# One tag per place: each tile goes where the kernel's own list schedule put it

## The chip, the cores and the metric

The kernel runs on one core of one Trainium2 chip. The metric is the device time of one execution in microseconds (us), as the median of several runs. The engines are named as in the profile: PE (TensorE, the matmuls; PEld its weight loads), DVE (VectorE), ACT (ScalarE), POOL (GpSimd) and SP (SyncE, which issues nearly all transfers here). PE writes its results into PSUM, which has eight banks of 2 KB per partition. All other tiles lie in SBUF.

## The reference

The input x has 2048 rows of 1024 bfloat16 numbers. Two layers with the same weights follow each other. A layer is an attention block A and then a feed-forward block B, each with a layer norm in front and a residual around it:

```
x = x + A(layernorm(x));  x = x + B(layernorm(x))        (twice)

A: qkv = x @ wqkv; 32 heads of 32 numbers
   position s looks at the 8 positions s, s-2, ..., s-14 (those that exist)
   o = softmax(q.k / sqrt(32)) v;  return o @ wo
B: h = relu(x @ w1 + b1)**2;  return h @ w2 + b2          (w1: 1024 x 3584)
```

## The kernel before

**Tiling.** A dilation of 2 keeps even and odd rows apart, so the rows are split by parity and worked on in blocks of 512: four blocks a layer, eight block steps u = 0 to 7 in all. A step has these stages: `SA` loads the rows and does the first layer norm; `SQ` or `SQ7` makes q, k and v; `S2` does the attention products on DVE; `SW` multiplies with wo, adds the residual (`xm`) and does the second layer norm; `SF1` and `SF2` are the two halves of the feed-forward block. Stages of neighbouring steps are interleaved: the attention of step u+1 runs on DVE while PE does the feed-forward block of step u.

**Seven products instead of eight.** From step 3 (q, k, v) and step 1 (feed-forward) on, a product of 2 x 2 blocks is made with seven block products, which share sums held in PSUM banks X, Y and Z (`product`; the matmul is line 572). Between products ACT copies a bank to SBUF, because the next product goes on adding to the same bank: a copy of X is a tile `u` (line 531 for q, k and v, lines 1060 and 1064 for the feed-forward block), a copy of Y or Z is `yq` (line 535) or `y` (line 1070). PE can't start the next product in that bank before the copy has been read out of it. DVE then adds `u` and `yq` (line 539). The combined weights are made once from the raw ones, in the early steps (`keep_w1`, `keep_wqkv` with tiles `tr` and `tv`, lines 464 and 469, and `keep_w2`), and are written to memory, from which later steps load them.

**Results.** `out_tile` adds a finished bank to `xm`: ACT copies the bank into a tile `yxo` (line 957), DVE adds and writes a tile `xo` (line 958), and SP stores `xo` to memory, to `xs` after the first layer and to the output after the second (line 353).

**What sets the order.** Nothing is left to an automatic scheduler. Every operation is recorded in a `Plan` with its engine, an estimated duration, a priority and the tiles that it reads and writes. `Plan.schedule` is a list scheduler: it goes forward in modelled time and gives each free engine its ready operation of the lowest priority number. The result is one order for all engines, in which `Plan.emit` then writes the instructions. On the chip each engine works through its own instructions in that order. Where one needs another engine's result, or a place that another tile still holds, it waits, and all behind it on its engine wait too. That holds for SP as well: a transfer that has to wait for its place holds back the transfers behind it.

**Places.** SBUF is divided into places of fixed sizes by class: 3 of 8304 bytes ("8Q": q, k, v), 11 of 8 KB ("8K": weights `w`, `xnA`, `xnB`, `o`, `s1`, T and TA), 6 of 4 KB, 12 of 2 KB ("2K": rows, `tr`, `tv`, `rr`), 9 of 1 KB ("1K": `u`, `y`, `yq`, `yxo`, `yxa`, `yxm`, `xo`), and some small ones. PSUM is the class "ps" with 8 places. The list scheduler keeps a list of free places for each class and starts an operation only when a place is free for each of its new tiles. It takes the place that has been free longest, and gives it back when the last user is done:

```python
b.slot = free[b.cls].pop(0)        # when the first user of tile b starts
free[b.cls].append(b.slot)         # when the last user of tile b is done
```

For a transfer, "done" is the end of its turn in a modelled queue of transfers (`DMA_MBS`, 0.38 MB a us) plus `DMA_LAT`, 2.2 us (or 4 us for the stores of combined weights). The number `b.slot` serves the plan alone. `place`, which `emit` calls when it writes the first instruction of a tile, asks a tile pool for the tile by the name of its class, with as many buffers as the class has places. The pool then chooses the place by its own rule as the instructions are written, and places the waits that this needs. So plan and program can differ in which tile follows which in a place.

Of the kernel before, what the change touches and what calls it, by code (L numbers as in the profile page):

```python
# [100 lines left out]
class Plan:  # L101
# [150 lines left out]
    def emit(self, place):  # L252
        self.shift(ORDER)
        order, self.timed = self.schedule()
        for o in order:
            for b in o.bufs:
                if b.tile is None:
                    b.tile = place(b)
            o.fn()

class _Kernel:
# [76 lines left out]

    def place(self, b):
        pool = self.psum if b.cls == "ps" else self.arena  # L340
        return pool.tile(b.shape, b.dt, name=b.tag, tag=b.cls, bufs=self.p.classes[b.cls][0])

    def nxt(self):
        self.seq += 1
# [995 lines left out]
```

## Time and profile before

| | us |
|---|---|
| median of 3 runs | 1171.28 |
| the three runs | 1168.42, 1171.89, 1171.28 |
| the profiled execution | 1168.59 |
| its span, first to last instruction | 1166.5 |

| in the span | busy | share | instructions |
|---|---|---|---|
| PE | 1145.8 us | 98% | 7572 |
| PEld | 767.6 us | 66% | 7623 |
| DVE | 1015.1 us | 87% | 1778 |
| ACT | 785.3 us | 67% | 1531 |
| 16 DMA engines, SP's queue | | 89.0% | 356.79 MB in all queues |

A wait in the profile is told as "engine, tile and line <- what ended it". A time of a matmul is modelled at its end, and neighbouring matmuls overlap, so the busy time of a group of matmuls is a little longer than the distance of their starts. A transfer is shown on its issuing queue (SPq) by the time of its issue. The time to its landing is counted from that issue. The granted clock is 1.00 where PE runs at full rate.

### The profile page before, as it was taken

Reading aid. Unit: us, or ns where it says so; the run is one execution under the profiler, and the core shown is the slowest. Engines: PE = TensorE matmul, PEld = TensorE weight load, DVE = VectorE, ACT = ScalarE, POOL = GpSimd, SP = SyncE. Lnnn points to the kernel's source line nnn. Section 1 sums busy time; section 2 is a strip of 40 time slices with the busy share of each in tenths; the row PEclk is TensorE's granted clock in tenths of the full one; section 3 lists DMA queues with packets and bytes.
Section 4 is the critical chain, followed back from the end, with each engine's and each line's share of the span. In section 5 each row is a group of like instructions: output and inputs, shape, how many; then the busy total and the mean of one; then the engine's idle time right before and its main releaser. Section 6 shows DMA issues by size and latency. Waiting matters only on the chain. (4 is left out here: it accounts for less than half of the span.)

```text
span 1166.5 us, 20203 instructions
## 1 busy us (share of the span) xinstructions
PE 1145.8 (98%) x7572; PEld 767.6 (66%) x7623; DVE 1015.1 (87%) x1778; ACT 785.3 (67%) x1531; POOL 1.8 (0%) x8
## 2 busy tenths in 40 slices
PE   8999999999999999999999999998999999999998
PEld 6565544557846787468864688555885568844864
DVE  4899999779999999959999699995999879998551
ACT  5743795565984689756894669845698376943771
POOL 0000000000000000000000000000000000000000
PEclk9999999999999999999999999999999999999999
DMA  9789999899999797997989797996979979787882
GB/s 353 215 238 285 348 282 313 292 315 343 379 327 382 230 382 256 342 383 237 371 287 372 263 358 272 298 395 209 368 258 323 406 246 386 248 327 273 294 291 90
DMA packets 196539, 356.79 MB, mean 306 GB/s; under 512 B 63834, under 2 KB 134874, under 8 KB 177242
## 3 DMA queue, kind: packets, MB, share of 16 engines
q1 hardware_dynamic: 196154, 354.99, 89.0%
q8 instruction: 59, 0.97, 0.3%
q10 hardware_dynamic: 288, 0.52, 0.1%
q14 instruction: 38, 0.31, 0.1%
HBM read 307.76 MB, written 39.58 MB: 298 GB/s over the span
## 5 line engine op out<-in xcount | busy, mean ns | idle before, releaser
L572 PEld LDWEIGHTS <-w 128*128 128x128 bf16 (+1 forms) x4424 | 433.3, 98 | 71.3 <-issue 10.6
L1153 PEld LDWEIGHTS <-r 128*128 128x128 f16 x1183 | 115.7, 98 | 134.4 <-ACT r L1091 0.8
L1153 PE MATMUL X<-w,r 128*128 128x512 f16 (+2 forms) x787 | 177.3, 377 | 0.3
L852 DVE TENSOR_TENSOR P<-q,k 128x2048 f16<-128x2048 f16 x128 | 154.1, 1223 | 12.4 <-ACT q L778 12.1
L931 DVE TENSOR_TENSOR pr<-pb,v 128x2048 f16<-128x2048 f16 x128 | 154.8, 1221 | 0.0
L572 PE MATMUL X<-T,w 128*128 128x256 f16 x1176 | 146.4, 273 | 0.2
L937 DVE TENSOR_TENSOR pr<-pr 128x512 f16<-128x512 f16 (+1 forms) x256 | 132.3, 550 | 0.0
L860 DVE TENSOR_TENSOR P<-P,P 128x2048 f16<-128x2048 f16 x102 | 123.7, 1217 | 0.1
L801 PE MATMUL pq<-xnA,w 128*128 128x512 f16 x528 | 118.0, 379 | 0.0
L982 PE MATMUL py<-w,o 128*128 128x512 bf16 x492 | 113.7, 380 | 3.1 <-ACT py L421 1.9
L1091 ACT ACTIVATE r<-rr 128x1024 f16<-128x1024 f16 x98 | 107.7, 1128 | 0.8 <-DVE rr L1083 0.5
L801 PEld LDWEIGHTS <-w 128*128 128x128 bf16 x528 | 75.3, 144 | 37.8
L572 PE MATMUL X<-TA,w 128*128 128x256 f16 x720 | 91.1, 274 | 5.3 <-ACT u L531 5.3
L982 PEld LDWEIGHTS <-o 128*128 128x128 bf16 x512 | 50.3, 98 | 59.0 <-issue 2.5
L531 ACT CAST u<-X 128x512 f16<-128x512 f32 x90 | 51.8, 589 | 46.2 <-PE X L572 32.8
L1074 DVE TENSOR_TENSOR rr<-u,y 128x512 f16<-128x512 f16 x147 | 60.9, 422 | 24.1 <-ACT y L1070 12.6
L1070 ACT CAST y<-Z 128x512 f16<-128x512 f32 x98 | 60.1, 637 | 14.3 <-PE Z L572 14.0
L643 DVE BATCH_NORM_STATS2 bs<-xm 128x6 f32<-128x512 f16 x64 | 43.9, 689 | 26.4 <-ACT xm L988 26.2
L1060 ACT CAST u<-X 128x512 f16<-128x512 f32 x105 | 62.5, 632 | 3.4 <-PE X L572 3.3
L988 ACT CAST xm<-py 128x512 f16<-128x512 f32 x52 | 30.5, 587 | 38.5 <-PE py L982 34.6
L572 PE MATMUL Z<-xnB,w 128*128 128x256 f16 x392 | 50.8, 273 | 0.0
L572 PE MATMUL Y<-xnB,w 128*128 128x256 f16 x392 | 50.6, 273 | 0.0
(133 smaller groups left out, 1629.9 us busy)
## 6 DMA issues: line engine op xcount, KB each, us to landing
w<-w1s SPq DMA_DIRECT2D x84, 1024.0 KB, 8.6
w<-tw SPq DMA_DIRECT2D x56, 896.0 KB, 6.5
w<-in_B_w_dram SPq DMA_DIRECT2D x42, 896.0 KB, 6.4
w<-wqqv SPq DMA_DIRECT2D x35, 1024.0 KB, 7.6
w<-in_A_wqkv_dram SPq DMA_DIRECT2D x18, 1024.0 KB, 8.6
w<-in_A_wo_dram SPq DMA_DIRECT2D x16, 1024.0 KB, 8.2
w<-wqk SPq DMA_DIRECT2D x15, 1024.0 KB, 8.5
w<-in_B_w_dram SPq DMA_DIRECT2D x28, 512.0 KB, 7.5
```

What stands on the lines that cost most here:

```text
L572: nc.tensor.matmul(bank[:, a, :], lw[:, k, left(a)], rhs(k), start=(start and k == 0 and a == 0), stop=(k == 3), skip_group_check=True)
L801: nc.tensor.matmul(pq[:], wv[:, kd % 4, c0:D:8], xnT[:, :, kd, :], start=(kd == 0), stop=(kd == KD - 1))
L852: nc.vector.tensor_tensor(cur[:], q[:, c, None, hb * HB:(hb + 1) * HB].to_broadcast([128, W, HB]), _win_ap(k[:, c, :], HALO + hb * HB, HB) ...
L860: nc.vector.tensor_tensor(other[:], other[:], cur[:], ALU.add)
L931: p.add("DVE", dve(2048), lambda pr=pr, ch=ch: nc.vector.tensor_tensor(pr[:], pb[:], _win_ap(v[:, ch, :], HALO + hb * HB, HB), ALU.mult), ...
L937: nc.vector.tensor_tensor(dst, pr[:, 0:n, :], pr[:, n:2 * n, :], ALU.add)
L982: nc.tensor.matmul(py[:], o[:, c, tl * 128:(tl + 1) * 128], wos[c // 4][:].rearrange("p (a b) n -> p a (b n)", a=4)[:, c % 4, db * 512:(db ...
L1060: p.add("ACT", act(512), lambda: nc.scalar.copy(us[i][:], X[:]), [(X, 0)], [(us[i], 0), (us[i], 1)], UP, name="u")
L1070: p.add("ACT", act(512), lambda: nc.scalar.copy(y[:], bank[:]), [(bank, 0)], [(y, 0)], 1.5, name="y")
L1074: p.add("DVE", dve(512), lambda: nc.vector.tensor_tensor(r[:, :, m, :], us[i][:], y[:], ALU.add), [(us[i], 0), (us[i], 1), (y, 0)], [(r, ( ...
L1091: p.add("ACT", act(1024), lambda: nc.scalar.activation(out=r2[:, f:f + 2, :].rearrange("p a t -> p (a t)"), in_=r[:].rearrange("p a m t -> ...
L1153: nc.tensor.matmul(banks[q][:, lo:hi], left(jj, q), w[:, j, lo:hi], start=(start and jj == 0), stop=(jj == h - 1), skip_group_check=True)
```

## The change

`place` now asks for the tile by a tag that names the class and the number `b.slot` that the list schedule gave the tile, with one buffer for each such tag. So the pool has nothing left to choose: each tile goes to the place that the plan gave it. The sizes and the number of places stay as they are. Their addresses in SBUF change, because the places are laid out in the order of their first use instead of class by class. The plan itself is not changed.

```diff
     def place(self, b):
         pool = self.psum if b.cls == "ps" else self.arena
-        return pool.tile(b.shape, b.dt, name=b.tag, tag=b.cls, bufs=self.p.classes[b.cls][0])
+        return pool.tile(b.shape, b.dt, name=b.tag, tag=f"{b.cls}.{b.slot}", bufs=1)
```

## The prediction

> **What bounds the kernel now.** I read the page's busy shares first, then who TensorE (PE) waits for, then the timeline around each of those waits, then windows over them, and last the tile view of the buffer found there. The page:
>
> ```profile
> PE 1145.8 (98%) x7572; PEld 767.6 (66%) x7623; DVE 1015.1 (87%) x1778; ACT 785.3 (67%) x1531; POOL 1.8 (0%) x8
> ```
>
> PE is busy for 98% of a span of 1166.5 us. Little can be won, and only where PE stands. The chain that ended last names matmuls almost alone. Next, the waits of PE alone (total, times, longest):
>
> ```profile
> PE X L572 <- ACT u L531: 5.3, 4, 2.1
> PE Z L572 <- ACT yq L535: 3.8, 1, 3.8
> PE py L982 <- ACT py L421: 1.9, 3, 0.7
> PE pt L717 <- DVE xn L699: 1.8, 1, 1.8
> ...
> PE Y L1153 <- ACT r L1091: 0.3, 1, 0.3
> ```
>
> No transfer is in this list: PE never waits for weights. The first two rows are five stalls. In each, PE wants a PSUM bank that ScalarE (ACT) has not copied out. Timeline of ACT at these five places; the bracket is its idle time and what ended it:
>
> ```profile
> 372.75 0.59 ACT L531 CAST u<-X 128x512 f16<-128x512 f32 x1 [2.68 <-DMA xs<-xo]
> ...
> 512.83 0.59 ACT L531 CAST u<-X 128x512 f16<-128x512 f32 x1 [2.16 <-DMA xs<-xo]
> ...
> 646.87 1.07 ACT L531 CAST u<-X 128x512 f16<-128x512 f32 x2 [2.18 <-DMA xs<-xo]
> ...
> 790.67 0.59 ACT L957 CAST yxo<-X 128x512 f16<-128x512 f32 x1 [5.06 <-DMA out_dram<-xo]
> ...
> 932.90 0.59 ACT L531 CAST u<-X 128x512 f16<-128x512 f32 x1 [4.34 <-DMA out_dram<-xo]
> ```
>
> The copy writes a 1 KB tile (u or yxo) into a place that an xo tile still holds, because its store to memory has not landed. The copy needs nothing from that store but the place. How slow the stores are, from the tile view of xo:
>
> ```profile
> DMA to landing us min/median/max: 1.6/5.3/10.9
> ```
>
> What one stall costs, from PE's timeline:
>
> ```profile
> 786.57 1.04 PE L572 MATMUL Y<-xnA,w 128*128 128x256 f16 x8
> 787.44 1.04 PE L572 MATMUL X<-TA,w 128*128 128x256 f16 x8
> ...
> 792.28 1.01 PE L572 MATMUL Z<-xnA,w 128*128 128x256 f16 x6 [3.81 <-ACT yq L535]
> ```
>
> Eight such matmuls start 0.87 us after the eight before (787.44 - 786.57). The next eight could start at 788.31 and start at 792.28: 3.97 us lost. There is a second loss behind it, in windows over the stall, the stretch after it, and the stall at 931 (PE, PEld, DVE, ACT, POOL, granted clock, DMA share, GB/s):
>
> ```profile
> 788.30:792.20 3.90, 0.17 (x2) 0.00 (x1) 0.00 (x0) 1.53 (x4) 0.00 (x0) 1.00 1.06 432
> 792.80:796.10 3.30, 3.08 (x15) 2.02 (x15) 0.83 (x3) 1.58 (x3) 0.00 (x0) 0.50 0.65 230
> ...
> 931.30:933.50 2.20, 0.13 (x2) 0.00 (x0) 0.00 (x0) 0.60 (x2) 0.00 (x0) 1.00 0.99 417
> ```
>
> After the stall of 3.97 us the granted clock is 0.50; the trace's clock records put that at 3.41 us. VectorE (DVE) has nothing to do in either stall: it is starved by them, not their cause.
>
> **The change part by part.** *Removed: five waits for a store.* By the rule of 787.44 above the losses of PE are: 370.92 + 0.87 = 371.79 to 373.39, 1.60; 511.58 + 0.87 = 512.45 to 513.47, 1.02; 645.54 + 0.87 = 646.41 to 647.50, 1.09; 3.97; 930.39 + 0.87 = 931.26 to 933.54, 2.28. Sum 9.96 us. All of it is on the path, since PE is the path.
>
> Do they go? The two built programs have the same instructions in the same order on every engine; waits and addresses differ. I laid the built addresses over the times of this trace. Of 2319 tiles that follow another tile in a place, 450 follow a different one. The five copies now follow tiles last read at 370.33, 510.20, 643.25, 785.86 and 929.02, all by DVE, no store. ACT became idle (start less bracket) at 370.07, 510.67, 644.69, 785.61 and 928.56, and the bank to be copied was complete at 370.21, 510.87, 644.83, long before, and 928.81. The latest of the three, plus 0.6 us, ends the copy at 370.9, 511.5, 645.4, 786.5 and 929.6, ahead of PE's 371.79, 512.45, 646.41, 788.31 and 931.26. At 788 PE needs the third of three copies, 0.48 us apart in the timeline: 787.5, a margin of 0.8 us, the smallest of the five. So all five go.
>
> *Removed with them: the slow clock.* 3.41 us at half rate do the work of 1.71 us: 1.7 us lost. The stall of 2.28 us left the clock at 1.00, so it goes even if the long stall only shrinks to that.
>
> *Late next.* Three copies stand on a store with little to spare before (0.25, 0.43 and 0.71 us after its landing); they move too. Over all 1 KB tiles the closest that the list's places come to a landed store, at these times, is 2.6 us (an xo written at 785.44).
>
> *Added: waits at the list's own places.* In 16 cases the tile now ahead in the place is still in use at the time of the write. Three kinds. (a) Seven weight loads from SP take the place of a tile that PE reads until 0.83 us (six) or 0.51 us (one) after the old issue. SP stands, and the loads, stores and transposes behind it in its queue stand too. Between 0, since these weights land 6.3 to 18.4 us ahead of their first reader, and 6 x 0.83 + 0.51 = 5.5 us if that lead were gone. I take 0: the lead is measured. (b) Where weights are combined and kept, 187 to 247 us: one ACT copy is 1.40 us late, two DVE operations 1.52 and 0.27, with PSUM copies queued behind the first and combinations behind the others. PE's three stalls there (239 to 252 us) sum to 0.87 + 0.59 + 0.89 = 2.35 us and end with ACT's seeding copies. Between -2.35, if other waits of ACT go and take these along, and +3.2. I take 0: the late copy is 50 us ahead of them, and the late DVE work does not end them. (c) Six ACT and DVE writes of 0.09 to 0.57 us: 0 to 0.6 for the one at 934, behind a stall that goes; the others are within 0.1. I take 0.
>
> *Sum.* The profiled execution took 1168.59 us (span 1166.5 and 2.1 around it). 1168.6 - 9.96 - 1.7 = 1156.9 us. It lies 2.7 us below the median of 1171.28 (runs 1168.42 to 1171.89). If those 2.7 us are stalls of these kinds they go too, if not they stay; I add 1.1 and say 1158.0.
>
> A rule that speaks against this: the Trainium skill, SBUF — State Buffer, "The DMA setup-cost knee", says that a transfer costs about a fixed 2 us plus its bytes over 436 GB/s. By it an xo store of 128 KB would take an estimated 2.3 us, the one issued at 780.92 would have left its place before 785.61, no copy would ever wait, and the change would be worth nothing: 1168.6. The trace disagrees: the copy at 790.67, 9.7 us after that issue, is released by its landing.
>
> **The rivals.** *New waits take back part.* For it: the kernel plans its list with 2.2 us to a landing (DMA_LAT) behind a modelled queue, where stores here take up to 10.9, so the list too can give a place that is not free. Against it: the rows under (a) to (c), and the nearest store at 2.6 us. All bounds at once are 5.5 + 3.2 + 0.6 = 9.3 us: 1166.2.
>
> *No gain: another resource sets the pace where the stalls were.* DVE is the candidate, at 87% overall and 98.6% busy from 260 to 371 us. Against it: 0.51 us of DVE work in 9.7 us of the five stalls. If PE ran into DVE each time, the time would stay at 1168.6. The same time results if the program does not do what it says, which the built addresses exclude.
>
> *Slower: the transfers become the bound.* From 376 to 1012 us the 16 DMA engines are 0.86 to 0.91 busy outside the stalls. Without 11.7 us of 641 the share becomes 0.88 to 0.93. The point is 1.0: if the moved places made the transfers there take 12% longer (570 us of work to 641), PE would start to wait for weights, and at 15% (656 us) the time would be 1168.6 + 15 = 1183. For it: the share reaches 1.03 in 260 to 371 us. Against it: PE loses 0.2 us in that very stretch.
>
> **How the numbers follow.** As forecast 0.72 (1154.5 to 1160); new waits take back part 0.14 (1160 to 1166); no gain 0.06 (1167.8 to 1174.8); slower 0.08. Range 1154.5 to 1166: the lower end is 1156.9 less the 2.35 of (b), the upper the bound of the first rival; it holds 0.86. A measurement of this kernel tells about 0.3%, 3.5 us, from no change: faster 0.86, same 0.06, slower 0.08.
>
> **What would show it.** Right: no transfer of xo among the releasers of ACT's u, yq and yxo copies; PE's rows for u and yq gone from its waits, or under 1 us; no clock of 0.50 between the start and the last slice; PE's matmul count and durations as before; SP's seven loads some 0.8 us later. Wrong: a new row in PE's waits over 1 us, most of all one ended by a transfer of weights, or a place at which a copy still waits for a store.

## The result, and the profile after

The changed kernel takes 1155.7 us (median of 4 runs, 1154.55 to 1156.4) against 1169.85 us for the kernel before in the same comparison (4 runs, 1168.01 to 1171.89). The ratio is 0.9878, with a 95% interval of 0.9855 to 0.9900. The forecast was 1158.0 us, in a range of 1154.5 to 1166.

The profiled execution of the changed kernel took 1156.19 us. The page's first lines:

```profile
span 1154.3 us, 20197 instructions
...
PE 1144.6 (99%) x7572; PEld 767.0 (66%) x7623; DVE 1014.6 (88%) x1778; ACT 786.4 (68%) x1531; POOL 1.8 (0%) x8
```

Every engine is busy for as long as before, to within 1.2 us. The span is 12.2 us shorter (1166.5 to 1154.3), and what went is time in which PE stood or ran at half its clock. The waits of PE (in total, times, longest):

```profile
PE pt L717 <- DVE xn L699: 1.2, 1, 1.2
PE pk L1259 <- DVE ones L287: 1.1, 1, 1.1
PE py L982 <- ACT py L421: 0.6, 1, 0.6
PE Y L1153 <- ACT r L1091: 0.3, 1, 0.3
```

The two rows that were first before, `X <- ACT u` (5.3 us) and `Z <- ACT yq` (3.8 us), are gone. No row took their place: still no transfer is among them. The row of `py` has shrunk from 1.9 us to 0.6. The five copies that had waited for a store, in ACT's timeline of the changed kernel:

```profile
369.85 0.59 ACT L531 CAST u<-X 128x512 f16<-128x512 f32 x1 [0.53 <-DVE k L539]
...
508.57 0.59 ACT L531 CAST u<-X 128x512 f16<-128x512 f32 x1 [0.23 <-PE X L572]
...
641.52 0.59 ACT L531 CAST u<-X 128x512 f16<-128x512 f32 x1 [0.18 <-PE X L572]
...
781.52 0.59 ACT L957 CAST yxo<-X 128x512 f16<-128x512 f32 x1 [0.29 <-DVE xo L958]
...
919.25 0.59 ACT L531 CAST u<-X 128x512 f16<-128x512 f32 x1 [0.62 <-DVE k L539]
```

In the brackets stand 0.2 to 0.6 us of idle time where 2.2 to 5.1 us stood, and what ends them is PE's own result or the last reader of the tile ahead in the place. The stores themselves have not become faster, as the tile view of xo shows:

```profile
who waited for it (us, times):
  ACT xm L988: 1.1, 1
  ACT yxo L957: 0.3, 1
...
DMA to landing us min/median/max: 1.6/5.6/10.8
```

A landing takes 5.6 us in the median (5.3 before). What changed is who stands behind it. Before, five copies waited for a store, 16.4 us in all. The two waits that the view of xo names now are of other kinds, as ACT's rows among the waits say:

```profile
ACT xm L988 <- DMA out_dram<-xo: 1.1, 1, 1.1
ACT yxo L957 <- DVE xo L958: 0.3, 1, 0.3
```

The `yxo` waited for DVE's addition and not for a transfer. An `xm` has a place of 2 KB, where no xo ever stands, so it shared no place with the store that ended its wait; what tied it to that store stays open. So in this execution no tile of 1 KB waited for a landing.

Sharing a place with a store has not ended with that. By the addresses in the built programs, 51 of ACT's copies follow an xo tile in a place before the change, and 47 after it. What has gone are the short distances: of the 1 KB writes behind a store whose landing the trace shows, the nearest now comes 3.1 us after it, where two `u` copies started 0.08 us after theirs before.

Last, windows over the same work as the stall at 788 us and the slow stretch behind it, 10 us earlier now (PE, PEld, DVE, ACT, POOL, granted clock, DMA share, GB/s):

```profile
782.60:786.50 3.90, 3.85 (x34) 3.12 (x33) 2.13 (x8) 2.83 (x5) 0.00 (x0) 1.00 1.07 437
786.60:789.90 3.30, 3.30 (x21) 1.86 (x19) 1.46 (x4) 2.08 (x4) 0.00 (x0) 1.00 1.04 437
```

PE is busy throughout, at a granted clock of 1.00; before it was busy for 0.17 us of the one and ran at 0.50 in the other.

Where the 12.2 us came from can be read by comparing the start of the same matmul in both traces:

| stretch of before, us | the changed kernel's lead at its end, us | gained in it, us |
|---|---|---|
| start to 238 | -0.16 | -0.16 |
| 238 to 260 (weights combined) | 0.97 | 1.13 |
| 260 to 371 | 0.74 | -0.23 |
| stall at 371 | 2.33 | 1.59 |
| stall at 511 | 3.35 | 1.01 |
| stall at 645 | 4.44 | 1.09 |
| stall at 788, with the slow clock | 10.08 | 5.64 |
| stall at 931, from 930 | 12.20 | 2.27 |
| the rest, and between the stalls | 12.20 | -0.14 |

The five stalls with the slow clock give 11.60 us of it.

### The profile page after: what moved, and what is told of

It reads as the page before. It is cut to its first block, busy times and chain, and to the rows that moved or that the text cites. A ratio compares the mean times of both kernels' runs of the same rounds, so it can differ in the third digit from the quotient of the medians.

```text
span 1154.3 us, 20197 instructions
## 1 busy us (share of the span) xinstructions
PE 1144.6 (99%) x7572; PEld 767.0 (66%) x7623; DVE 1014.6 (88%) x1778; ACT 786.4 (68%) x1531; POOL 1.8 (0%) x8
## 3 DMA queue, kind: packets, MB, share of 16 engines
q1 hardware_dynamic: 196154, 354.99, 89.9%
## 5 line engine op out<-in xcount | busy, mean ns | idle before, releaser
L852 DVE TENSOR_TENSOR P<-q,k 128x2048 f16<-128x2048 f16 x128 | 154.2, 1223 | 12.4 <-ACT q L778 12.1
L982 PE MATMUL py<-w,o 128*128 128x512 bf16 x492 | 113.4, 379 | 1.8 <-ACT py L421 0.6
L982 PEld LDWEIGHTS <-o 128*128 128x128 bf16 x512 | 50.0, 98 | 57.6 <-DVE sm L652 0.9
```

Source lines behind the costliest of these rows:

```text
L852: nc.vector.tensor_tensor(cur[:], q[:, c, None, hb * HB:(hb + 1) * HB].to_broadcast([128, W, HB]), _win_ap(k[:, c, :], HALO + hb * HB, HB) ...
L982: nc.tensor.matmul(py[:], o[:, c, tl * 128:(tl + 1) * 128], wos[c // 4][:].rearrange("p (a b) n -> p a (b n)", a=4)[:, c % 4, db * 512:(db ...
```

## Experiments: which class of places does it

Two runs split the change. The first gives the list's places to the 1 KB class alone:

```diff
-        return pool.tile(b.shape, b.dt, name=b.tag, tag=f"{b.cls}.{b.slot}", bufs=1)
+        return pool.tile(b.shape, b.dt, name=b.tag, **({"tag": f"{b.cls}.{b.slot}", "bufs": 1}
+            if b.cls == "1K" else {"tag": b.cls, "bufs": self.p.classes[b.cls][0]}))
```

> Only the 1 KB class gets the list's places, one tag for each; every other class is left to the pool as before. Theory (all of the gain is five copies that no longer land in a place whose last user is a store of xo, 9.96 us of waits, with 1.7 us of slow clock behind the longest): these five waits and the slow clock are gone, and the three waits of TensorE in the stage where the weights are combined (239 to 252 us, 0.87, 0.59 and 0.89 us before) stay as they were, since their tiles are of other classes. That is 1168.6 - 11.7 = about 1157 us for an execution like the profiled one of before, a ratio of 0.989 to 0.991, about 1.1 us above the changed kernel. Rival (the places of the large classes are needed too): the five waits shrink by half or less, ratio 0.994 or more.

Measured: 1157.16 us, ratio 0.9883 (0.9864 to 0.9902). The rows for `u` and `yq` are gone from PE's waits, and the row of the weight stage stands about as before (1.9 us there):

```profile
PE py L982 <- ACT py L421: 1.7, 3, 0.7
PE pt L717 <- DVE xn L699: 1.7, 1, 1.7
PE pk L1259 <- DVE ones L287: 1.1, 1, 1.1
PE Y L1153 <- ACT r L1091: 0.3, 1, 0.3
```

So the 1 KB class is enough for the gain. Read by the starts of the matmuls, as in the table above, the run gains 11.6 us at the five stalls and 0.1 us from 238 to 260 us. The time is the 1157 us expected; the ratio came out a little under the 0.989 expected, since the kernel before is slower in most executions than in its profile (below).

The second run does the opposite, all classes but this one:

```diff
+        ... if b.cls != "1K" else ...
```

> Every class but the 1 KB one gets the list's places; the 1 KB class is left to the pool as before. Theory: the five waits of TensorE for copies at about 371, 511, 645, 788 and 931 us stand again (1.60, 1.02, 1.09, 3.97 and 2.28 us, within some tenths) and the slow clock behind the fourth; only the waits at 239 to 252 us fall, from 2.35 to about 1.2 us. So 1.1 us less than before: a ratio of 0.998 to 1.000. Rival (the 1 KB class is not the one that matters): a ratio of 0.988 to 0.992 as the full change.

Measured: 1155.93 us, ratio 0.9873 (0.9854 to 0.9892). That is the whole gain as well, and the theory as it stood fell. PE's waits of this run:

```profile
PE pt L717 <- DVE xn L699: 1.2, 1, 1.2
PE pk L1259 <- DVE ones L287: 1.1, 1, 1.1
PE py L982 <- ACT py L421: 0.6, 2, 0.4
PE pq L801 <- ACT yxo L957: 0.6, 1, 0.6
PE Y L1153 <- ACT r L1091: 0.3, 1, 0.3
```

The five waits are gone although the pool still picks the 1 KB places. The addresses in the built program tell why: the pool did not pick what it had picked before. In 171 cases a different tile is ahead in a 1 KB place, and none of the five copies follows a store any more. The pool's choice in this class changed with the tags of the others. So this run did not undo what it was meant to undo; what was needed was the old 1 KB places themselves, written out.

## Experiments: the old places, with nothing else undone

From the kernel before, the place of each of the 700 tiles of 1 KB was written down, in order, as a table of 700 digits. Every other class has the list's places:

```diff
+OLD = ("0812734560812734560812734560813247560813274560183275..."
+       ...)
+def old_1k(self, b):
+    if b.cls != "1K":
+        return b.slot
+    self.n1k = getattr(self, "n1k", -1) + 1
+    return OLD[self.n1k]
...
+        return pool.tile(..., tag=f"{b.cls}.{old_1k(self, b)}", bufs=1)
```

> The changed kernel with the 700 places of the 1 KB class as the pool had picked them in the kernel before, written out as a table; every other class has the list's places. This is what the run with every class but the 1 KB one by the list was meant to be: there the pool picked 171 of the 1 KB places otherwise than before, and none of the five copies stood behind its store. Theory: the five waits of before stand again, 9 to 10 us, with the slow clock, and only the 1.1 us at 239 to 252 us are kept: a ratio of 0.997 to 1.000, equal to the run with the five exchanges within 0.002. Rival (the large classes' places bring the gain by themselves, which is how that run came out): 0.987 to 0.990.

The other run goes to the core of it. It is the changed kernel, but at five points two 1 KB places change names, so that the five copies follow the same stores as before:

```diff
+BACK = {("u", 24): ("xo", 12), ("u", 64): ("xo", 20), ("u", 100): ("xo", 28),
+        ("yxo", 39): ("xo", 36), ("u", 181): ("xo", 44)}
+def swapped(self, b):
+    ...
+    back = BACK.get((b.tag, n))        # n: the number of this tile among those of its name, from 0
+    if back:                           # from here on, exchange this tile's place and the store's
+        at, here = self.held[back], self.swap[b.slot]
+        there = next(i for i in self.swap if self.swap[i] == at)
+        self.swap[b.slot], self.swap[there] = at, here
+    ...
```

> The changed kernel, with five exchanges of two places, so that the five copies named before (four u and one yxo) land again behind the very stores that they stood behind in the kernel before; all other 1 KB tiles and all other classes have the list's places, apart from the names that the exchanges carry on. Theory (these five make the whole difference): TensorE waits five times, 1 to 4 us each and 8 to 10 us in all, with a slow clock behind the longest: 10 to 12 us over the changed kernel, a ratio to before of 0.997 to 1.000, only the 1.1 us at 239 to 252 us kept. Rival (waits do not add up, since a kernel that was held up once has its stores landed by the next time): under 6 us over the changed kernel, ratio below 0.994. Second rival (other places of the 1 KB class matter as well): the same, from too small a loss.

Measured, with the kernel before at 1169.2 us beside both:

| | us, median of 12 | ratio to before |
|---|---|---|
| five copies back behind their stores | 1166.32 | 0.9976 (0.9964 to 0.9989) |
| all 1 KB places as before | 1165.27 | 0.9971 (0.9953 to 0.9989) |
| the changed kernel again, same chip, an earlier comparison | 1156.77 (6 runs) | 0.9889 (0.9864 to 0.9915) |

The third row was measured ahead of these two, as the mark for two other runs, with this expectation:

> The changed kernel once more, beside the two others on the same chip, as the mark for them. A ratio to before of 0.986 to 0.990; if the two experiments lie within 0.001 of it they count as equal.

Against the changed kernel, the five exchanges change which tile is ahead for ten tiles: the five copies, and five that come later in the exchanged places. They alone cost 9.6 us, a little under the 10 to 12 us expected, and the 700 old places cost no more than they. PE's waits with the five exchanges, and ACT's timeline at the longest:

```profile
PE X L572 <- ACT u L531: 5.6, 4, 2.2
PE Z L572 <- ACT yq L535: 3.6, 1, 3.6
PE py L982 <- ACT py L421: 1.2, 2, 0.7
...
```

```profile
791.91 0.58 ACT L957 CAST yxo<-X 128x512 f16<-128x512 f32 x1 [4.83 <-DMA out_dram<-xo]
```

The rows of before are back to within 0.3 us (5.3 with four, 3.8 with one). The rival that the waits would not add up is out, and so, within the intervals of some 2 us either way, is the rival that other 1 KB places matter: both runs end at the same ratio within 0.001. A third rival, that the tiles' new addresses in SBUF bring the gain, is out as well: the run with the five exchanges has the same set of addresses as the changed kernel, and the time of before is nearly back. Five exchanges of places make most of the 12.4 us by which the changed kernel was faster than before on this chip (1169.2 - 1156.8). Neither run returns quite to 1.000; the mean of the two is 0.997, 3 us short. About 1 us of that is the weight stage, where the list's places stay (below). The rest was not separated: the waits with the 700 old places were also shorter in the one execution that was profiled (4.3 and 2.5 us in the two rows).

## Experiments: one wait at a time

Two runs put back one copy each, by the same exchange of two places, to see whether the price of one wait is as it was worked out. First the longest, at 788 us:

```diff
+    ...
+    if (b.tag, n) == ("xo", 36):
+        self.held = b.slot
+    if (b.tag, n) == ("yxo", 39):
+        self.swap = {b.slot: self.held, self.held: b.slot}
+    ...
```

> The changed kernel, but from one copy (the yxo of block 39) on, its place of 1 KB and that of one store's tile (the xo of block 36) are exchanged, so that this one copy lands again where it did before. Theory: TensorE waits once at about 778 us (the same work that stood at 788 us before) for 4.0 us, and the clock then falls to half for some microseconds, which costs 1.7 us more: 5.7 us over the changed kernel, a ratio to before of 0.992 to 0.994, against 0.988 for the changed kernel. Rival (the wait only moves, since something else is late anyway): the wait stands, but the time rises by less than 2 us. Second rival: the wait is there and the clock stays at full speed: 4.0 us over.

Measured: 1161.94 us in the median of 6, ratio 0.9921 (0.9899 to 0.9942), as expected. But the six runs are not of one kind: two took 1158.10 and 1159.02 us, four took 1161.84 to 1162.93. The profiled one is that of 1159.02, and in it PE's wait is shorter and the clock stays at full rate (the waits, then windows over the wait and behind it):

```profile
PE Z L572 <- ACT yq L535: 2.7, 1, 2.7
...
```

```profile
784.20:786.90 2.70, 0.06 (x1) 0.00 (x0) 0.00 (x0) 1.51 (x4) 0.00 (x0) 1.00 1.06 436
787.10:790.40 3.30, 3.25 (x23) 2.25 (x24) 1.46 (x4) 2.00 (x4) 0.00 (x0) 1.00 0.79 268
```

By the starts of its matmuls that wait cost 2.9 us, and 1156.2 + 2.9 is 1159.1. The other four lie some 3.5 us higher, and were not profiled. A longer wait and the slow clock would make most of that together (1.1 + 1.7 = 2.8 us for the wait of before). The mean clock fits this in three of them, with 0.998 or 0.999, as one slow stretch leaves it. It does not fit the fourth, which took 1162.05 us at 1.000, so what made that one longer stays open. The price of this one sharing was 2 to 7 us over the changed kernel's 1155.7.

Then the copy at 931 us, whose wait of 2.28 us had left the clock alone:

```diff
+    if (b.tag, n) == ("xo", 44): ...
+    if (b.tag, n) == ("u", 181): ...
```

> As the run before, for another copy (the 181st u, on the place of the 44th xo). Theory: TensorE waits once at about 919 us for about 2.3 us, and its clock stays at full speed, since the 2.28 us wait of before was not followed by a slow record: 2.3 us over the changed kernel, a ratio to before of 0.989 to 0.991. Rival (any wait of this kind brings the slow clock): 4.0 us over.

Measured: 1158.61 us, ratio 0.9894 (0.9877 to 0.9911). One wait of 2.2 us stands in PE's row, at a clock of 1.00:

```profile
PE X L572 <- ACT u L531: 2.2, 1, 2.2
...
```

The changed kernel was not run beside it. The time is 1.8 us over the 1156.77 that it took on another chip and 2.9 over its first 1155.7, around the 2.3 expected. The intervals of the ratios (0.9878 for the changed kernel) overlap, so it is the wait in the profile that shows this price, and the times only agree with it.

## Experiments: is it the store, or the list's places?

If the cause is that a copy shares a place with a store, then it is enough to keep the stores' tiles apart. The kernel before, with the pool choosing everywhere, but three extra places of 1 KB for xo alone:

```diff
+        return pool.tile(b.shape, b.dt, name=b.tag, **({"tag": "xo", "bufs": 3}
+            if b.tag == "xo" else {"tag": b.cls, "bufs": self.p.classes[b.cls][0]}))
```

> The kernel before, with the pool's own choice of places everywhere, but the tiles of the xo store have a class of their own with three more buffers of 1 KB, so that no copy of TensorE's path can follow a store in a place. The list's places are not used. Theory (the cause is the sharing of a place with a store, and not the list's places as such): the five waits for copies and the slow clock go, 11.7 us, and the waits at 239 to 252 us stay: about 1157 us, a ratio of 0.988 to 0.991. Rival (the list's places do something more): the five waits go in part or others come, a ratio of 0.993 or more.

Measured: 1155.95 us, ratio 0.9881 (0.9858 to 0.9904). The list's places are not used at all, and the gain is the same. PE's waits:

```profile
PE pk L1259 <- DVE ones L287: 1.1, 1, 1.1
PE py L982 <- ACT py L421: 1.0, 1, 1.0
PE pt L717 <- DVE xn L699: 0.8, 1, 0.8
PE Y L1153 <- ACT r L1091: 0.3, 1, 0.3
```

The wait for the store has not vanished, as the tile view of xo shows. It has moved to DVE, which now waits twice for one of the three places:

```profile
who waited for it (us, times):
  DVE xo L958: 8.6, 2
...
```

These 8.6 us on DVE cost PE nothing that its waits show. The run changes more than it names: there are three more places, and the pool, choosing anew, put a different tile ahead of some 300 of the 700 tiles of 1 KB. So it agrees with the cause and shows that the list is not needed; that the five copies are the cause rests on the five exchanges.

The other direction, to see whether better places than the list's are to be had: the changed kernel, with the list taking the place that has been free longest, and counting a place last used by a transfer as free 8 us later.

```diff
-        free = {c: list(range(n)) for c, (n, _) in self.classes.items()}
+        free = {c: [(-1.0, i) for i in range(n)] for c, (n, _) in self.classes.items()}
...
-                        b.slot = free[b.cls].pop(0)
+                        b.slot = free[b.cls].pop(free[b.cls].index(min(free[b.cls])))[1]
...
-                                free[b.cls].append(b.slot)
+                                free[b.cls].append((t + (8.0 if o.mb else 0.0), b.slot))
```

> The changed kernel, with the list choosing, of the free places of a class, the one that has been free longest, where a place last used by a transfer counts as free 8 us later than the list thinks. Theory: the two waits that are left behind a store (xm 1.1 us, yxo 0.3 us, neither of which holds up TensorE by more than some tenths) go, and TensorE's 4.4 us of waits hardly change: the changed kernel's time within 1 us, a ratio to before of 0.987 to 0.989. Rival (the new order of places brings a copy behind a late load): 1 to 4 us over the changed kernel.

Measured: 1155.76 us, ratio 0.9878 (0.9855 to 0.9901), against 0.9889 (0.9864 to 0.9915) for the changed kernel beside it. The two ratios differ by 0.0011, hardly more than the 0.001 that was to count as equal, and the intervals lie over each other: no gain and no loss that could be told. The expectation took the waits of `xm` and `yxo` (1.1 and 0.3 us) for waits behind a store's place, which they were not; in this run one `yxo` does wait for a store, for 0.9 us, and no wait of PE is put down to it. PE waits for little now that a place could mend.

## Experiment: the kernel before, profiled again

> The kernel before once more, for a second profile of it. Theory: the same five copies wait, but for times that differ by a microsecond or more from those of the first profile, since the stores land at other times in each execution; how many of the waits are long enough for the slow clock differs with them, and so the time, 1166 to 1173 us. Rival: the waits are the same to some tenths, and the spread of the times of before has another cause.

Measured: 1169.47 us, with a mean granted clock of 0.997 against 0.999 in the first profile. The waits of PE for the copies, and windows over two of the waits with the stretch behind each:

```profile
PE X L572 <- ACT u L531: 4.9, 3, 2.4
PE Z L572 <- ACT yq L535: 3.6, 1, 3.6
...
```

```profile
644.40:647.10 2.70, 0.40 (x4) 0.20 (x3) 0.00 (x0) 0.56 (x2) 0.00 (x0) 1.00 1.02 423
647.70:650.90 3.20, 3.20 (x17) 2.21 (x16) 2.07 (x6) 1.47 (x3) 0.00 (x0) 0.50 0.93 341
789.70:793.40 3.70, 0.11 (x2) 0.00 (x0) 0.00 (x0) 1.55 (x4) 0.00 (x0) 1.00 1.05 434
794.50:797.70 3.20, 2.98 (x11) 1.62 (x11) 1.03 (x3) 1.17 (x2) 0.00 (x0) 0.50 0.77 259
```

The same program, and yet the wait at 371 us is missing, because that store landed 2 us earlier:

```profile
370.56 0.58 ACT L531 CAST u<-X 128x512 f16<-128x512 f32 x1 [0.68 <-DMA xs<-xo]
```

The wait at 645 us is 2.54 us instead of 1.09, and there are two stretches at half clock instead of one. So the waits do differ from one execution to the next, as expected, but not each of them by a microsecond: two of the five do, and the other three lie within 0.4 us. The 45 timed executions of the kernel before that were run beside the experiments show the same by their mean clock, in which one stretch of 3.41 us at half rate makes 1.7 of 1167 us, or 0.0015:

| mean clock | executions | mean time, us |
|---|---|---|
| 1.000 | 2 | 1167.8 |
| 0.999 and 0.998 (about one stretch) | 16 | 1168.5 |
| 0.997 and 0.996 (two or more) | 27 | 1171.0 |

The last row lies 2.5 us above the one before it, more than the 1.7 us of one stretch; longer waits would make the rest, which no profile here separates. In each of the changed kernel's ten executions the clock is 1.000.

## Why the prediction was right

*The five waits and the slow clock.* Forecast as 9.96 + 1.7 = 11.66 us. Measured between the two profiles: 1.59, 1.01, 1.09, 5.64 with the slow clock, and 2.27, together 11.60. One step about the clock was weaker than it read: that a stall of 2.28 us left the clock at 1.00 does not mean that such a stall is safe. The 2.28 us lay across a border of the clock's grid, and 2.29 us within one window of it were enough for the slow clock in another run (last section). Since all five stalls went, nothing hung on this step. That they come from five copies behind stores is shown by the five exchanges, which bring them back (9.6 us), and by the places of their own for xo, which take them away without the list.

*Late next.* The smallest margin, 0.8 us at 788 us, held. So did the statement that no 1 KB tile of the list's places comes near to a landed store: 2.6 us was the closest by the times of the profile before, and 3.1 us in the profile after.

*New waits (a), seven weight loads.* Taken as 0, between 0 and 5.5 us. No wait for weights is among PE's in the profile after, so the seven delays stayed hidden behind the lead of the loads: right. The delays themselves are there: measured against the matmuls around it, the load issued at 672.87 us before is issued 0.86 us later now.

*New waits (b), the weight stage at 187 to 247 us.* Taken as 0 with bounds from -2.35 to +3.2; measured as a gain of 1.13 us. This is the term that was mis-sized. One profile would be thin for it, but PE's row `py L982 <- ACT py L421` stands in all but two of the twelve (0 in the table):

| places of the classes other than 1 KB | that row's total in each profile, us | mean |
|---|---|---|
| the pool's (before, before again, only 1 KB by the list, xo apart) | 1.9, 1.6, 1.7, 1.0 | 1.55 |
| the list's (the eight others) | 0.6, 0.6, 0.7, 0, 0.9, 0, 1.2, 0.4 | 0.55 |

So the list's places of these classes are worth 1.0 us of this wait in the mean, though the two groups overlap. The starts of the matmuls say the same: from 238 to 260 us the first group gains 0 to 0.9 us on the first profile of before (mean 0.3), the second 0.65 to 2.34 (mean 1.4). The late operations that were listed under (b) cost PE nothing there. No operation that comes earlier had been costed; that those are the gain follows only by exclusion, and which of them it is stays open.

*The offset of the median.* 1.1 us of the 2.7 us between the profiled execution and the median were left standing. They went nearly whole. The first profile of before is one with about one slow stretch; by the table of clocks, executions with two or more are the commonest and 2.5 us longer (1171.0 against 1168.5), and with the waits for stores their slow stretches go as well. The changed kernel has none, and its times lie closer together: 1154.55 to 1156.4. The two terms together, 1.1 of (b) and 1.1 left standing, make nearly all of the 2.3 us between the 1158.0 forecast and the 1155.7 measured.

*The rivals.* The gain was not taken back by new waits, since the kernel is 2.3 us faster than forecast, not slower. DVE did not set the pace: its share rose from 87% to 88%, and with 8.6 us more waiting for the store in one experiment PE was no later. The transfers did not become the bound: SP's queue has a share of 89.9% instead of 89.0%, and no wait of PE is for one.

*A part that stays open* is by what rule the pool set the five copies behind stores. In the kernel before, all five took a place whose last user in the order of the instructions was the issue of a store, while the list gave them a place whose last reader stood later in that order but was done earlier. In the run with the 1 KB class left to the pool, it chose otherwise, and no run showed what it goes by.

## What to carry to other kernels

When a transfer is the last user of a small place, the place comes free when the transfer lands, here 1.6 to 11 us behind its issue and 5.3 in the median, and not when it is issued; a copy on the busiest engine's path must not be the next tenant so soon. Sharing alone does no harm: the changed kernel keeps 47 such successions, and its copies come late enough. Look at what ends the waits of the copies that empty PSUM: if it is a store with which the copy has nothing else in common, a few buffers of the store's own are enough (three of 1 KB here), without any change to the order of work. An undo that leaves a pool its freedom may undo nothing, so compare the addresses in the built programs before such a run is read.

## What was not expected of the hardware

*Whether a wait brings the slow clock depends on where it falls.* A wait of 2.54 us (before, second profile) and one of 2.71 us (all old 1 KB places) were each followed by the slow clock, and the wait of 2.91 us (one copy back at 788 us) was not. Windows over the wait of 2.71 us and the stretch behind it:

```profile
786.90:789.50 2.60, 0.10 (x1) 0.00 (x0) 0.00 (x0) 1.57 (x4) 0.00 (x0) 1.00 0.98 402
790.40:793.70 3.30, 3.08 (x13) 1.84 (x13) 1.08 (x4) 1.25 (x3) 0.00 (x0) 0.50 0.77 281
```

Each slow record lasts 3.413 us, but for the one that the end of the trace cuts short, and in the second profile of before 143.36 us lie between the end of the first and the start of the second, which is 42 times 3.413. So the clock is set on a fixed grid. The Trainium skill, TensorE: Matmul & The Clock Gate, "What's actually happening", says that activity is judged in windows of 3413 ns that run freely; the distances in the trace agree. Laid over that grid, the waits that were followed by the slow clock left PE idle for 2.93 (before), 2.54 and 2.51 (before again), 2.63 (old 1 KB places) and 2.29 us (five copies back) of the 3.41 us ahead of the slow record. The wait of 2.91 us lay across a border, with 1.37 us in one window and 1.54 in the next. The same section says that the slow clock comes after at least one idle window; in these profiles two thirds of one were enough. Less was not: waits of 1.87 us, each within one window (at 932 us, in before again and with the five copies back), were not followed by the slow clock. Where the grid had no record near a wait, its place was carried on from the next record, so these last figures are worked out and not read.

*The landing of a store differs from one execution to the next by microseconds.* The store ahead of the copy at 371 us landed at about 372.7 us in one profile of before and at about 370.5 in the other, with the same program, and with ACT idle before the copy from 370.07 and 369.88 us on, so at the same point of the work to within 0.2 us.
